# One pool of eight PSUM banks for score pairs and single-bank users, loads ordered on one queue, Q evacuated for both parities in one operation

## The chip, the cores and the metric

The kernel runs on one core of one Trainium2 chip. The metric is the time of one execution on the device in microseconds (us), taken as the median of several runs. Engines are named as in the profile: PE (TensorE matmuls), PEld (its weight loads), DVE (VectorE), ACT (ScalarE), POOL (GpSimd), SP (the queue that issues most loads).

## The reference, cut to what matters

Two branches on an input of 2048 tokens by 512 features, mixed by a gate per token:

```python
g = sigmoid((x * gate_w).sum(-1, keepdims=True))
a = A_ref(x, wqkv, wo)      # attention: 32 heads of 16, causal, window of 256 tokens
b = B_ref(x, w1, b1, w2, b2)     # layernorm, then an MLP over the tokens
return g * a + (1 - g) * b
# A_ref: q, k, v = x @ wqkv; softmax(q k^T / 4, masked) v; @ wo
# B_ref: u = gelu(einsum("bsd,sf->bdf", layernorm(x), w1) + b1); y = einsum("bdf,fs->bds", u, w2) + b2
```

What matters here is the shape of the work. The projections make Q, K and V. Attention runs in 90 *groups*: one block of 128 queries, half the heads, one block of 128 keys. A group is 8 small score matmuls into PSUM, two exps on ACT of 128x1024 each, and 16 small matmuls with V. The MLP has a *first product* (176 matmuls of 512 columns, needs the layernorm of all tokens) and a *second product* (176, needs all of the first and the weight w2, which is loaded into the place of w1 when the first product is over).

## The kernel before

All work is cut into tasks; a planner inside the program (`arrange`) walks through them with assumed durations and fixes one order of instructions for every engine before anything runs. A task may take buffers of a *ring*; the planner decides which buffer of the ring it gets. The framework then puts in the semaphores, from what each instruction reads and writes. So the order is fixed, and an instruction that has to wait holds up everything behind it on its engine.

The parts that the change and the argument touch (cuts marked `# ...`):

```python
    def ring(name, n, shape, dtype, space):
        pool = psum if space == "psum" else sb
        return Ring(name, [pool.tile(shape, dtype, name=f"{name}{i}") for i in range(n)])

    sp = ring("sp", 3, [P, 1024], FP32, "psum")     # three pairs of banks, for scores
    gp = ring("gp", 2, [P, 512], FP32, "psum")      # two single banks, for everything else
    # ...
    def chain(name, mms, deps, prio, piece=2):      # a sum of matmuls, in pieces of two
        b = gp.use()
    # ...
                for p in range(2):                  # Q, once for each parity, on ACT or DVE
                    q.append(copy_out(
                        f"qc{k}_{i}{p}", lambda k=k, p=p: QZ[:, i % NQ, p, k, :], lambda b=b: buf(b)[:],
                        [t, k4] + free_q.get((k, i - NQ), []), 4, b, 0.53, scale=par[:, p:p + 1],
                    ))
    # ...
            b2 = [sp.use(), sp.use()]               # one group takes two of the three pairs
            # ...
            s = add(f"s{qb}.{hf}.{kb}", {"PE": 0.40}, emit_s, need, 1 + 0.001 * slot, takes=b2)
            ex = []
            for j in range(2):
                ex.append(add(
                    f"e{qb}.{hf}.{kb}.{j}", {"ACT": 0.96},
                    lambda j=j, b2=b2, e=e: nc.scalar.activation(
                        out=buf(e)[:, j * 1024:(j + 1) * 1024], in_=buf(b2[j])[:], func=ACT.Exp, scale=SCALE
                    ),
                    [s] + ex, 6 + 0.001 * slot, takes=[e] if j == 0 else [], uses=[b2[j]] + ([e] if j else []),
                ))
```

PSUM is the memory that PE writes its sums to. A *bank* is a piece of it with 512 fp32 values per partition, and both kernels divide PSUM into eight of them: here three pairs and two single banks. Every user of a single bank (transposes, projections, products with V, both MLP products, the output projection) is called a *single* below.

The softmax here doesn't subtract the row's maximum and nothing guards it: scores larger than these inputs give would overflow.

## Time and profile before

270.6 us (269.3 to 271.5). The profiled execution is a slightly longer one, 274.3 us, with a span of 272.2 us on the core. The kernel falls into six stages with different limits. I cut the trace at landmarks: first score matmul, first and last matmul of the first product, first of the second product, last score matmul.

| stage | us | what limits it |
|---|---|---|
| start | 18.7 | loads, then cold matmuls |
| A: projections and attention | 46.3 | DVE, ACT, PE about equally |
| first product | 89.6 | PE |
| wait for w2 | 21.5 | ACT |
| second product | 71.7 | ACT |
| tail | 24.4 | PE alone |

The first fence has the head of the page of the kernel before: the span, and the busy time of each engine.

```profile
span 272.2 us, 6817 instructions
PE 239.9 (88%) x2968; PEld 118.4 (43%) x2968; DVE 145.8 (54%) x256; ACT 214.2 (79%) x255; POOL 68.5 (25%) x50
```

The second has the same kernel by stage: for each stretch its length, then busy time and count of each engine, the granted clock of PE, the share of the DMA engines and GB/s.

```profile
core 0: us, PE busy (x) PEld busy (x) DVE busy (x) ACT busy (x) POOL busy (x), PEclk, DMA share, GB/s
0.00:18.70 18.70, 12.47 (x68) 5.53 (x69) 8.44 (x22) 3.54 (x5) 8.27 (x16) 0.82 0.94 258
18.70:65.00 46.30, 37.46 (x470) 17.86 (x470) 38.21 (x75) 38.12 (x48) 9.74 (x9) 0.93 0.29 110
65.00:154.60 89.60, 84.31 (x1072) 41.71 (x1069) 51.50 (x81) 76.65 (x94) 22.38 (x11) 0.96 0.06 20
154.60:176.10 21.50, 19.03 (x262) 9.91 (x261) 12.07 (x19) 20.21 (x27) 4.01 (x2) 1.00 0.49 186
176.10:247.80 71.70, 67.84 (x981) 34.70 (x981) 29.70 (x50) 69.54 (x78) 22.05 (x11) 1.00 0.06 20
247.80:272.20 24.40, 18.77 (x128) 8.69 (x127) 5.90 (x11) 6.12 (x8) 2.00 (x1) 0.99 0.10 33
```

Read it by rows: in the second product ACT is busy 69.54 of 71.70, and in the last row nobody but PE has much to do. These 18.8 us of PE work come too late.

The third has the waits of PE and ACT of the kernel before that bear on PSUM buffers: who waited for whom, us in total, how often, the longest.

```profile
ACT et L474 <- PE sp L457: 2.7, 6, 1.2
...
PE sp L457 <- ACT et L474: 1.3, 4, 0.5
...
PE gp L356 <- DVE on L534: 4.3, 8, 0.7
PE gp L356 <- ACT QZ L313: 4.2, 5, 1.3
...
PE gp L356 <- DVE QZ L317: 1.7, 3, 0.7
```

The hand-over between scores and exps costs almost nothing (2.7 and 1.3 us in 90 groups). Over all its lines PE waits 14.2 us for DVE and 8.5 us for ACT.

### The profile page before, as it was taken

The page shows a single profiled execution, that of the slowest core. Times are in us where ns is not written, and L with a number is a line of the kernel's source. Part 1 is how long each engine was busy: PE and PEld are TensorE (multiplying, and loading weights), DVE is VectorE, ACT ScalarE, POOL GpSimd, SP SyncE. Part 2 cuts the span into 40 slices and gives each one's busy share as a digit, 9 for nine tenths or more (in the row PEclk, how much of TensorE's full clock was granted, in tenths as well). Part 3 has the DMA queues.
Part 4 walks back from the last instruction along what each step waited for, and adds up shares of the span by engine and source line. Part 5 has one row for each costly group of instructions (what it writes and reads, how often), then busy time and mean ns, then how long its engine had stood idle before and what let it go on. Part 6 is the DMA issues. An engine that isn't in the chain of part 4 may idle for free.

```text
span 272.2 us, 6817 instructions
## 1 busy us (share of the span) xinstructions
PE 239.9 (88%) x2968; PEld 118.4 (43%) x2968; DVE 145.8 (54%) x256; ACT 214.2 (79%) x255; POOL 68.5 (25%) x50
## 2 busy tenths in 40 slices
PE   5588888888989999998798989899998989899894
PEld 1243443434455455444433534445454444444431
DVE  0679977785566554758524574525425253443222
ACT  0239969689988977999569899999999999997221
POOL 8300403041340222131202221133333322222000
PEclk9689979799997999999989999999999999999999
DMA  6999600000000000000000992001001010101001
GB/s 212 214 386 404 235 0 2 1 2 0 2 2 2 0 2 0 2 2 2 1 0 4 363 411 60 0 2 41 4 19 39 5 39 2 41 0 41 22 19 58
DMA packets 9757, 18.00 MB, mean 66 GB/s; under 512 B 672, under 2 KB 5792, under 8 KB 9728
## 3 DMA queue, kind: packets, MB, share of 16 engines
q1 hardware_dynamic: 8512, 15.99, 16.5%
q10 hardware_dynamic: 1056, 1.57, 2.0%
q8 instruction: 23, 0.38, 0.6%
q0 software_dynamic: 160, 0.01, 0.5%
q14 instruction: 6, 0.05, 0.1%
HBM read 15.47 MB, written 2.10 MB: 65 GB/s over the span
## 4 chain that ended last, share of the span: by engine, by line
PE 56%; ACT 20%; DVE 15%; issue 4%; DMA 4%; DVEq 0%; ACTq 0%
PE gp L356 41%; ACT et L474 12%; PE sp L457 7%; PE gp L512 7%; DMA wqkv<-in_A_wqkv_dram 4%; DVE QZ L317 3%; DVE et L483 3%; ACT QZ L313 3%; ACT bp L637 2%; DVE h L423 2%; DVE on L534 2%; DVE ug L611 1%; ACT uf L589 1%; DVE rd L527 1%; PE gp L548 1%
## 5 line engine op out<-in xcount | busy, mean ns | idle before, releaser
L474 ACT ACTIVATE et<-sp 128x1024 bf16<-128x1024 f32 x180 | 171.6, 1045 | 4.2 <-PE sp L457 2.7
L492 POOL TENSOR_SCALAR_AFFINE_SELECT et<-et 128x2048 bf16<-128x2048 bf16 x28 | 56.6, 2021 | 151.7 <-ACT et L474 131.7
L512 PEld LDWEIGHTS <-et 128*128 128x128 bf16 x1440 | 46.1, 96 | 23.6 <-issue 14.2
L483 DVE TENSOR_TENSOR et<-et,mask 128x2048 bf16<-128x2048 bf16 x32 | 39.1, 1223 | 31.5 <-ACT et L474 31.2
L512 PE MATMUL gp<-VA,et 128*128 128x17 bf16 x1440 | 48.2, 171 | 4.2 <-DVE QZ L317 1.1
L356 PE MATMUL gp<-h,wb 128*128 128x512 bf16 (+1 forms) x176 | 47.6, 386 | 0.0
L356 PE MATMUL gp<-ug,wb 128*128 128x512 bf16 (+1 forms) x176 | 44.5, 379 | 2.7 <-DVE on L534 2.6
L356 PEld LDWEIGHTS <-wb 128*128 128x128 bf16 (+2 forms) x352 | 29.9, 98 | 35.2 <-issue 10.9
L356 PE MATMUL gp<-XT,wqkv 128*128 128x512 bf16 x128 | 38.1, 420 | 8.1 <-DMA wqkv<-in_A_wqkv_dram 2.3
L457 PE MATMUL sp<-QZ,KT 32*128 32x256 bf16 x720 | 41.3, 277 | 3.5 <-ACT et L474 1.3
L457 PEld LDWEIGHTS <-KT 32*128 32x128 bf16 x720 | 13.3, 92 | 37.1 <-issue 35.8
L637 ACT ACTIVATE bp<-gp,c,c 128x512 f32<-128x512 f32 x16 | 12.4, 779 | 16.5 <-PE gp L356 16.1
L356 PE MATMUL gp<-wqkv,XT 128*128 128x512 bf16 x64 | 19.3, 407 | 3.8 <-ACT QZ L313 2.5
L527 DVE RECIPROCAL rd<-gp 128x16 f32<-128x16 f32 x32 | 8.1, 254 | 26.0 <-PE gp L512 15.2
L356 PEld LDWEIGHTS <-wqkv 128*128 128x128 bf16 x128 | 11.9, 103 | 22.8 <-issue 13.0
L313 ACT ACTIVATE QZ<-gp,par 128x512 bf16<-128x512 f32 x18 | 12.2, 692 | 10.5 <-DVE QZ L317 6.2
L356 PE MATMUL gp<-wo,xo 128*128 128x512 bf16 x64 | 17.7, 377 | 1.8 <-ACT bp L637 1.0
L645 DVE SCALAR_TENSOR_TENSOR ot<-gp,gg,bp 128x512 bf16<-128x512 f32 x16 | 11.9, 748 | 13.7 <-PE gp L356 12.4
L317 DVE TENSOR_SCALAR QZ<-gp,par 128x512 bf16<-128x512 f32 x14 | 10.5, 750 | 15.2 <-ACT QZ L313 8.8
L594 DVE TENSOR_TENSOR t<-uf 128x512 f32<-128x512 f32 (+1 forms) x11 | 8.1, 738 | 12.3 <-ACT uf L589 12.3
L534 DVE TENSOR_TENSOR on<-gp,rd 128x256 bf16<-128x256 f32 x32 | 13.6, 424 | 1.1
L406 DVE BATCH_NORM_STATS2 stats<-xo 128x6 f32<-128x512 bf16 x16 | 10.4, 681 | 5.5 <-DMA xo<-in_A_x_dram 5.5
(49 smaller groups left out, 129.8 us busy)
## 6 DMA issues: line engine op xcount, KB each, us to landing
wb<-in_B_w_dram SPq DMA_DIRECT2D x4, 1376.0 KB, 17.1
wb<-in_B_w_dram SPq DMA_DIRECT2D x3, 1536.0 KB, 8.0
xo<-in_A_x_dram SPq DMA_DIRECT2D x4, 512.0 KB, 12.9
out_dram<-ot SPq DMA_DIRECT2D x16, 128.0 KB, 1.7
wqkv<-in_A_wqkv_dram ACTq DMA_DIRECT2D x1, 1024.0 KB, 9.8
wqkv<-in_A_wqkv_dram ACTq DMA_DIRECT2D x1, 512.0 KB, 13.3
wo<-in_A_wo_dram SPq DMA_DIRECT2D x1, 512.0 KB, 16.3
wb<-in_B_w_dram SPq DMA_DIRECT2D x1, 512.0 KB, 11.6
```

The lines of the kernel that those rows point to most:

```text
L313: nc.scalar.activation(out_(), in_(), ACT.Copy, scale=scale)
L317: nc.vector.tensor_scalar(out=out_(), in0=in_(), scalar1=scale, scalar2=None, op0=ALU.mult)
L356: nc.tensor.matmul(buf(b)[:rows, :], lhsT=lhsT, rhs=rhs, start=(j == 0), stop=(j == n - 1))
L457: nc.tensor.matmul(buf(b2[r // 2])[:, (r % 2) * 512 + kk * 256:(r % 2) * 512 + kk * 256 + 256], lhsT=KT[32 * r:32 * r + 32, (kb // 4) % NK ...
L474: lambda j=j, b2=b2, e=e: nc.scalar.activation(out=buf(e)[:, j * 1024:(j + 1) * 1024], in_=buf(b2[j])[:], func=ACT.Exp, scale=SCALE),
L483: lambda e=e: nc.vector.tensor_tensor(out=buf(e)[:].rearrange("p (n q) -> p n q", q=P), in0=buf(e)[:].rearrange("p (n q) -> p n q", q=P), ...
L492: lambda e=e: nc.gpsimd.affine_select(out=buf(e)[:], in_=buf(e)[:], pattern=[[0, 16], [-1, P]], compare_op=ALU.is_gt, fill=0.0, base=0, ch ...
L512: nc.tensor.matmul(buf(o)[:, hl * DV:(hl + 1) * DV], lhsT=buf(e)[:, col:col + 128], rhs=VA[:, kb, head, :], start=(first and hl == 0), sto ...
L527: lambda rd=rd, o=o: nc.vector.reciprocal(out=buf(rd)[:], in_=buf(o)[:, 0:16 * DV].rearrange("p (h d) -> p h d", d=DV)[:, :, DH]),
L534: lambda rd=rd, o=o, ob=ob, hf=hf: nc.vector.tensor_tensor(out=buf(ob)[:, hf * 256:(hf + 1) * 256].rearrange("p (h d) -> p h d", d=DH), in ...
L637: lambda bp=bp, b=b, qb=qb: nc.scalar.activation(buf(bp)[:], buf(b)[:], ACT.Identity, bias=c2[:, qb:qb + 1], scale=c1[:, qb:qb + 1]),
L645: lambda bp=bp, b=b, ot=ot, qb=qb: nc.vector.scalar_tensor_tensor(out=buf(ot)[:], in0=buf(b)[:], scalar=gg[:, qb:qb + 1], in1=buf(bp)[:], ...
```

## The change

Its intent: let singles have up to four banks, so that PE always finds a bank for a filler between scores; bring the first loads in sooner; take Q's evacuation off ACT. Four parts:

1. **Pool.** PSUM becomes four tiles of two banks each. A group takes two whole tiles; a single takes one half of tile 2 or 3 (banks 4 to 7).
2. **Loads** go through one queue in the order x0, wqk, x1, wv, x2, x3.
3. **Q** is evacuated by one DVE operation for both parities.
4. **Planner**: an exp is assumed to take 0.905 us, not 0.96; a group may not be planned before the start of the first exp of the group ahead of it; the exp table is loaded at the start.

```diff
-    sp = ring("sp", 3, [P, 1024], FP32, "psum")
-    gp = ring("gp", 2, [P, 512], FP32, "psum")
+    ps = Banks("ps", [0.0] * 8)
+    pst = [psum.tile([P, 1024], FP32, name=f"ps{i}") for i in range(4)]
 ...
     def buf(b):
-        return b.ring.tiles[b.index]
+        if b.ring is not ps:
+            return b.ring.tiles[b.index][:]
+        t = pst[b.index // 2]
+        return t[:] if b.size == 2 else t[:, (b.index % 2) * 512:(b.index % 2 + 1) * 512]
+
+    ANY = (4, 5, 6, 7)
 ...
+    load_x(0)
+    dwk = load_w("wqk", 0, 2 * D, 0.005)
+    load_x(1)
+    dwv = load_w("wv", 2 * D, 3 * D, 0.015)
+    load_x(2)
+    load_x(3)
 ...
-                for p in range(2):
-                    q.append(copy_out(
 ...
+                q = [add(
+                    f"qc{k}_{i}", {"DVE": 1.25},
+                    lambda k=k, b=b: nc.vector.tensor_tensor(
+                        out=QZ[:, i % NQ, :, k, :], in0=buf(b)[:, None, :].to_broadcast([P, 2, SB]),
+                        in1=par[:][:, :, None].to_broadcast([P, 2, SB]), op=ALU.mult,
+                    ),
+                    [t, k4], 4, uses=[b],
+                )]
 ...
-            b2 = [sp.use(), sp.use()]
+            b2 = [ps.use(2), ps.use(2)]
 ...
-            s = add(f"s{qb}.{hf}.{kb}", {"PE": 0.40}, emit_s, need, 1 + 0.001 * slot, takes=b2)
+            s = add(f"s{qb}.{hf}.{kb}", {"PE": 0.40}, emit_s, need, 1 + 0.001 * slot, takes=b2, after=prev)
 ...
-                    f"e{qb}.{hf}.{kb}.{j}", {"ACT": 0.96},
+                    f"e{qb}.{hf}.{kb}.{j}", {"ACT": 0.905},
```

(Cut: the class `Banks`, which prefers low tiles for groups and high banks for singles, and the wait of a projection chain for the last reader of the K or Q that it will replace.)

More of the change, by code (lines that the diff above doesn't have):

```diff
@@ L14, with __init__ @@
 class Buf:
-    def __init__(self, ring):
+    def __init__(self, ring, size=1, banks=None):
         self.ring = ring
+        self.size = size
+        self.banks = banks
         self.index = None
@@ L31, in use, with when, take, give @@
         return Buf(self)
+    def when(self, bufs):
+        times = sorted(x for x in self.avail if x is not None)
+        return times[len(bufs) - 1] if len(times) >= len(bufs) else None
+    def take(self, bufs, start):
+        for b in bufs:
+            b.index = min((i for i, x in enumerate(self.avail) if x is not None), key=lambda i: self.avail[i])
+            self.avail[b.index] = None
+    def give(self, b):
+        self.avail[b.index] = b.end
+class Banks(Ring):
+    def use(self, size=1, banks=None):
+        return Buf(self, size, banks)
+    def when(self, bufs):
+        a = self.avail
+        if bufs[0].size == 2:
+            times = sorted(
+                max(a[i], a[i + 1]) for i in range(0, len(a), 2) if a[i] is not None and a[i + 1] is not None
+            )
+        else:
+            times = sorted(x for i, x in enumerate(a) if x is not None and i in bufs[0].banks)
+        return times[len(bufs) - 1] if len(times) >= len(bufs) else None
+    def take(self, bufs, start):
+        a = self.avail
+        for b in bufs:
+            if b.size == 2:
+                free = [i for i in range(0, len(a), 2) if a[i] is not None and a[i + 1] is not None]
+                b.index = min(free, key=lambda i: (max(a[i], a[i + 1]) > start, i))
+                a[b.index] = a[b.index + 1] = None
+            else:
+                free = [i for i in b.banks if a[i] is not None]
+                b.index = min(
+                    free, key=lambda i: (a[i] > start, a[i ^ 1] is not None and a[i ^ 1] <= start, -i)
+                )
+                a[b.index] = None
+    def give(self, b):
+        for i in range(b.index, b.index + b.size):
+            self.avail[i] = b.end
 class Task:
-    def __init__(self, name, engines, emit, deps=(), prio=50.0, lat=None, takes=(), uses=(), at=0.0):
+    def __init__(self, name, engines, emit, deps=(), prio=50.0, lat=None, takes=(), uses=(), after=()):
         self.name = name
@@ L45, in __init__ @@
             b.users += 1
-        self.at = at
+        self.need = {}
+        for b in self.takes:
+            self.need.setdefault(b.ring, []).append(b)
+        self.after = [(d, s) for d, s in after if d is not None]
         self.done = None
@@ L49, in __init__ @@
         self.next = []
-        self.ready = at
+        self.ready = 0.0
 LATENCY = {"PE": 0.22, "ACT": 0.15, "DVE": 0.12, "POOL": 0.15, "SP": 2.0}
@@ L58, in arrange @@
     for t in tasks:
-        t.left = len(t.deps)
+        t.left = len(t.deps) + len(t.after)
         for d in t.deps:
-            d.next.append(t)
+            d.next.append((t, None))
+        for d, s in t.after:
+            d.next.append((t, s))
     free = {e: 0.0 for e in LATENCY}
@@ L78, in arrange @@
                 start = max(free[e], t.ready)
-                need = {}
-                for b in t.takes:
-                    need[b.ring] = need.get(b.ring, 0) + 1
-                for ring, n in need.items():
-                    times = sorted(x for x in ring.avail if x is not None)
-                    start = max(start, times[n - 1]) if len(times) >= n else None
-                    if start is None:
+                for ring, bufs in t.need.items():
+                    at = ring.when(bufs)
+                    if at is None:
+                        start = None
                         break
+                    start = max(start, at)
                 if start is not None:
@@ L106, in arrange @@
         t.start = start
-        for b in t.takes:
-            ring = b.ring
-            b.index = min(
-                (i for i, x in enumerate(ring.avail) if x is not None), key=lambda i: ring.avail[i]
-            )
-            ring.avail[b.index] = None
+        for ring, bufs in t.need.items():
+            ring.take(bufs, start)
         for b in t.takes + t.uses:
@@ L116, in arrange @@
             if not b.users:
-                b.ring.avail[b.index] = b.end
+                b.ring.give(b)
         order.append(t)
-        for n in t.next:
+        for n, s in t.next:
             n.left -= 1
-            n.ready = max(n.ready, t.done)
+            n.ready = max(n.ready, t.done if s is None else start + s)
             if not n.left:
@@ L210, in buf, with bank @@
     def buf(b):
-        return b.ring.tiles[b.index]
+        if b.ring is not ps:
[3 more added lines that the diff above has]
+    ANY = (4, 5, 6, 7)
+    def bank(banks=ANY):
+        return ps.use(1, banks)
     tasks = []
@@ L218, in add @@
         return t
-    landed = [2.2]
+    landed = [2.3]
     def load(name, emit, kb, q="SP", deps=(), prio=0.0, small=None):
-        landed[0] += kb / 330.0
+        landed[0] += kb / 370.0
         lat = small if small is not None else landed[0]
@@ L228, with load_x, emit, load_w @@
     dx = []
-    dx.append(load("x0", lambda: nc.sync.dma_start(xo[:, 0:4, :], X[0:SB].rearrange("(t p) d -> p t d", p=P)), 512))
-    dwk = load(
-        "wqk",
-        lambda: nc.scalar.dma_start(wqkv[:, :, 0:2 * D], A_wqkv[:, 0:2 * D].rearrange("(c p) n -> p c n", p=P)),
-        1024, q="ACT",
-    )
-    dwv = load(
-        "wv",
-        lambda: nc.scalar.dma_start(wqkv[:, :, 2 * D:3 * D], A_wqkv[:, 2 * D:3 * D].rearrange("(c p) n -> p c n", p=P)),
-        512, q="ACT", prio=0.1,
-    )
-    for i in range(1, NSB):
-        def emit(i=i):
-            nc.sync.dma_start(xo[:, 4 * i:4 * i + 4, :], X[i * SB:(i + 1) * SB].rearrange("(t p) d -> p t d", p=P))
-        dx.append(load(f"x{i}", emit, 512, prio=0.1 * i))
+    def load_x(i):
+        def emit():
+            nc.sync.dma_start(xo[:, 4 * i:4 * i + 4, :], X[i * SB:(i + 1) * SB].rearrange("(t p) d -> p t d", p=P))
+        dx.append(load(f"x{i}", emit, 512, prio=0.01 * len(dx)))
+    def load_w(name, a, z, prio):
+        return load(
+            name, lambda: nc.sync.dma_start(wqkv[:, :, a:z], A_wqkv[:, a:z].rearrange("(c p) n -> p c n", p=P)),
+            z - a, prio=prio,
+        )
+    load_x(0)
[4 more added lines that the diff above has]
+    load_x(3)
     dw1 = []
@@ L297 @@
     k6 = add("biases", {"DVE": 0.35}, biases, [k3], prio=30)
-    wu = gp.use()
+    add("table", {"ACT": 1.4}, lambda: nc.scalar.activation(th[:, 0:1], eps[:, 0:1], ACT.Exp), [k0], prio=0)
+    wu = bank()
     warm = add(
@@ L327 @@
         for c in range(2):
-            b = gp.use()
+            b = bank()
             def emit(i=i, c=c, b=b):
-                g16 = buf(b)[:].bitcast(BF16)
+                g16 = buf(b).bitcast(BF16)
                 for cc in range(2):
@@ L341, with chain @@
                 lambda i=i, c=c: XT[:, 2 * c:2 * c + 2, i * SB:(i + 1) * SB],
-                lambda b=b: buf(b)[:].bitcast(BF16).rearrange("p (c s) -> p c s", c=2),
+                lambda b=b: buf(b).bitcast(BF16).rearrange("p (c s) -> p c s", c=2),
                 [t], 5 + i, b, 0.53, both=False,
             )
-    def chain(name, mms, deps, prio, piece=2):
-        b = gp.use()
+    def chain(name, mms, deps, prio, piece=2, banks=ANY):
+        b = bank(banks)
         n = len(mms)
@@ L383, in project @@
             ]
-            b, t = chain(f"{kind}{k}_{i}", mms, [dwk, xt[i, 0], xt[i, 1], warm], prio)
+            old = free_k.get((k, i - NK), []) if kind == "k" else free_q.get((k, i - NQ), [])
+            b, t = chain(f"{kind}{k}_{i}", mms, [dwk, xt[i, 0], xt[i, 1], warm] + old, prio)
             if kind == "k":
@@ L387, in project @@
                     f"kc{k}_{i}", lambda k=k: KT[:, i % NK, k, :], lambda b=b: buf(b)[:],
-                    [t] + free_k.get((k, i - NK), []), 4, b, 0.53,
+                    [t], 4, b, 0.53,
                 )
             else:
-                q = []
-                for p in range(2):
-                    q.append(copy_out(
-                        f"qc{k}_{i}{p}", lambda k=k, p=p: QZ[:, i % NQ, p, k, :], lambda b=b: buf(b)[:],
-                        [t, k4] + free_q.get((k, i - NQ), []), 4, b, 0.53, scale=par[:, p:p + 1],
-                    ))
+                q = [add(
[6 more added lines that the diff above has]
+                )]
                 qready[k, i] = q
@@ L437 @@
     SCALE = DH ** -0.5
+    LEAD = 0.0
+    prev = []
     slot = 0
@@ L470 @@
             ex = []
+            prev = []
             for j in range(2):
                 ex.append(add(
-                    f"e{qb}.{hf}.{kb}.{j}", {"ACT": 0.96},
+                    f"e{qb}.{hf}.{kb}.{j}", {"ACT": 0.905},
                     lambda j=j, b2=b2, e=e: nc.scalar.activation(
@@ L478 @@
                 ))
+            prev = [(ex[0], LEAD)]
             got = ex
@@ L499 @@
             slot += 1
-        o = gp.use()
+        o = bank()
         last = None
@@ L542 @@
         if len(rel[qb]) == 2:
-            tb = gp.use()
+            tb = bank()
             def emit_t(tb=tb, ob=ob):
@@ L554 @@
             )
-    gb = gp.use()
+    gb = bank()
     def emit_gate():
```

## The prediction

> **What bounds the kernel now.** No one engine throughout. By windows cut at landmarks of the timeline (first score, first and last matmul of the first MLP product, first of the second, last score):
>
> - 0-18.7 us, start: loads. The chain of waits begins with the load of wqkv to 10.6 us. The next 12 matmuls take 0.43 us each, half clock (later 0.22).
> - 18.7-65, projections and attention (A): DVE busy 40 of 46, ACT 40, PE 39.5 (hand-offs of two single banks).
> - 65-154.6, first product: PE 82.
> - 154.6-176, waiting for w2: ACT 20 of 21.5.
> - 176-247.8, second product: ACT 69.5 of 71.7.
> - 247.8-272.2, tail: PE alone, 18.8 of 24.4; five second-product chains are left after the last exp.
>
> Busy (page): PE 239.9, ACT 214.2, DVE 145.8. My sum of warm PE work is 229; some 43 us go to the start, hand-offs and clock (granted 0.96).
>
> **What the change does.**
> 1. Loads: x0, then wqk, then x1, on one queue. Today x0 lands at 7.2 and wqk at 10.6, sharing the engines. At the timeline's 210-290 GB/s x0 should land near 5, wqk near 8.2: 2-2.5 us sooner. The early table load was hidden already.
> 2. Q: 18 ACT (0.69) and 14 DVE (0.75) evacuations become 16 DVE operations, estimated at 1.2 us from the 0.75. ACT loses 12.4 us, DVE gains 9. Today the pair runs in series (waits: DVE on ACT 8.8 us, ACT on DVE 6.2). The Trainium skill, "PSUM — Partial Sum Buffer", Terms, says that two engines may not access one bank at once, reads included; the trace agrees: 1.44 us back to back. The bank is released at most 0.25 us sooner.
> 3. Banks: singles get four banks instead of two; scores mostly the other two pairs. In the built order most score groups reuse pairs 0 and 1, so a group waits for the previous group's second exp; three pairs let it wait for the first only. Estimated 0.6-0.8 us of ACT gap each, unless another ACT operation fills it.
> 4. Order: score groups are held back, fillers come forward. In the built order, groups by stage go from 17/32/8/33 to 29/23/10/28, 512-column matmuls after the last score from 75 to 39.
>
> **On the critical path.** Warm PE work per stage (trace durations) plus losses like today's: start 16.8; A has 62 of PE, 65 of ACT, 65 of DVE: 72; first product 62 of PE: 66; w2 gap, ten groups of exps: 20.5; second product 70.5 of PE, 63.5 of ACT plus gaps: 73.5; tail 10.4 plus 4: 14. Sum near 263. The gain is mainly the tail, about 10 us, and the start, 2; A, with more on DVE, and the two-pair hand-off give some back.
>
> **Predicted 262 us**, range 253 to 269. Faster by over 2%: 0.68; within 2%: 0.28; slower: 0.04.
>
> **What would show it.** First k chain at 8-8.5 us; first exp near 17.5; Q operation 1.15-1.25 us; ACT busy near 201, DVE near 155; first product from 88; last exp 14 us before the end; waits of scores on exps up from 1.3 us, of exps on scores from 2.7, to several us; waits of chains on QZ and on `on` down from 10.
>
> **What would make it wrong.** The two-pair hand-off stalling both PE and ACT on each group (268-275). DVE limiting A, so that the first product starts after 95. Or four single banks removing nearly all PE stalls, with a clock that warms earlier (the skill, "TensorE: Matmul & The Clock Gate", Part 1: about 3.4 us of sustained work; in the trace half clock holds until 15 us): 250.

## More of the kernel before

Each ratio compares a kernel with the kernel before on the same chip in the same rounds; two variants that ran in different rounds are compared by these ratios.

## The result, and the profile after

The changed kernel takes 307.6 us (305.6 to 309.7) against 270.5 us: ratio 1.1375, 95% interval 1.128 to 1.147. It is 37 us slower. (A ratio here is the mean time of one kernel's fast runs over the mean of the other's of the same rounds, so it is not quite the ratio of the medians.)

The page of the changed kernel begins:

```profile
span 308.0 us, 6790 instructions
PE 241.0 (78%) x2921; PEld 122.0 (40%) x2968; DVE 161.0 (52%) x259; ACT 207.2 (67%) x237; POOL 71.9 (23%) x50
```

PE is about as busy as before (241.0 against 239.9 us, though 47 of its 2968 matmuls have no record in this trace), and ACT is less busy. Nearly all of the 36 us of span is waiting: over all lines PE waits 59.4 us, before 27.4. By stage, with the same landmarks:

```profile
core 0: us, PE busy (x) PEld busy (x) DVE busy (x) ACT busy (x) POOL busy (x), PEclk, DMA share, GB/s
0.00:19.40 19.40, 12.47 (x77) 6.62 (x79) 8.91 (x20) 2.68 (x4) 8.28 (x16) 0.91 0.95 264
19.40:113.70 94.30, 68.55 (x884) 34.81 (x898) 62.06 (x109) 60.29 (x70) 19.19 (x13) 0.89 0.13 51
113.70:184.10 70.40, 61.81 (x763) 30.95 (x776) 44.15 (x60) 57.60 (x69) 16.58 (x8) 1.00 0.09 30
184.10:208.40 24.30, 16.12 (x265) 8.83 (x267) 12.94 (x17) 19.36 (x22) 6.16 (x3) 0.75 0.40 151
208.40:290.60 82.20, 71.38 (x861) 35.47 (x876) 29.06 (x48) 63.04 (x69) 19.67 (x9) 0.97 0.06 21
290.60:308.00 17.40, 10.70 (x89) 5.28 (x91) 3.87 (x7) 4.28 (x5) 2.01 (x1) 0.93 0.09 32
```

In stage A no engine is at its limit: 68.55, 62.06 and 60.29 of 94.30. The tail did shrink, as planned, from 24.4 to 17.4 us. The waits that answer to those shown of before (L418 is now the line of the chains, L581 that of the products with V, L524 the scores, L542 the exps):

```profile
ACT et L542 <- PE ps L524: 38.2, 39, 3.3
...
PE ps L418 <- DVE QZ L456: 8.9, 9, 1.9
...
PE ps L418 <- DVE ot L714: 6.1, 9, 1.7
...
PE ps L418 <- DVE on L603: 5.9, 10, 0.8
...
PE ps L581 <- DVE QZ L456: 3.6, 3, 1.5
...
PE ps L524 <- ACT et L542: 2.6, 7, 0.5
```

Over all its lines PE now waits 41.7 us for DVE (before: 14.2) and 13.5 us for ACT (8.5). That is odd: the singles have twice the banks, and PE waits almost three times as long for DVE, which is one of the two engines that read them. The waits of scores on exps stay small (2.6 us), while exps wait 38.2 us for scores.

A stretch of the timeline of the changed kernel, in the first product, shows how odd. Columns: start, length, engine, line, operation, output and input, count, and in brackets the idle time before and what ended it.

```profile
130.67 0.55 PE L581 MATMUL ps<-VA,et 128*128 128x17 bf16 x16
...
131.08 1.96 PE L418 MATMUL ps<-h,wb 128*128 128x512 bf16 x8
131.71 0.26 DVE L596 RECIPROCAL rd<-ps 128x16 f32<-128x16 f32 x1 [0.47 <-PE ps L418]
...
132.32 2.01 POOL L561 TENSOR_SCALAR_AFFINE_SELECT et<-et 128x2048 bf16<-128x2048 bf16 x1 [6.94 <-ACT et L542]
132.65 0.42 DVE L603 TENSOR_TENSOR on<-ps,rd 128x256 bf16<-128x256 f32 x1 [0.68 <-PE ps L418]
...
132.99 1.88 DVE L680 SCALAR_TENSOR_TENSOR ug<-t,uf 128x512 bf16<-128x512 f32 x1
```

The last product with V (L581) ends near 131.2. Its readers are the reciprocal and the multiplication (L596, L603). Neither can start then; both wait for matmuls of the first product (L418), which write another bank. Nothing in the reference makes them depend on each other. What they share is the two-bank tile: in the built program this reciprocal reads the lower half of tile 3 and carries a wait on a matmul of the first product that writes the upper half.

### The profile page after: what moved, and what is told of

Read it like the earlier page. It is cut to its first block, busy times and chain, and to the rows that moved or that the text cites. A ratio compares the mean times of both kernels' runs of the same rounds, so it can differ in the third digit from the quotient of the medians.

```text
span 308.0 us, 6790 instructions
## 1 busy us (share of the span) xinstructions
PE 241.0 (78%) x2921; PEld 122.0 (40%) x2968; DVE 161.0 (52%) x259; ACT 207.2 (67%) x237; POOL 71.9 (23%) x50
## 4 chain that ended last, share of the span: by engine, by line
PE 54%; DVE 25%; ACT 11%; issue 6%; another core or an unknown queue 2%; DVEq 0%; ACTq 0%
PE ps L418 36%; PE ps L581 9%; DVE QZ L456 6%; ACT et L542 5%; PE ps L524 5%; DVE ot L714 4%; DVE on L603 3%; ACT bp L706 2%; DVE et L552 2%; DVE h L488 2%; ACT uf L658 2%; DVE xo L621 1%; DVE rd L596 1%; DVE VA L377 1%
## 5 line engine op out<-in xcount | busy, mean ns | idle before, releaser
L542 ACT ACTIVATE et<-ps 128x1024 bf16<-128x1024 f32 x180 | 174.3, 1025 | 39.0 <-PE ps L524 38.2
L581 PEld LDWEIGHTS <-et 128*128 128x128 bf16 x1440 | 48.1, 97 | 32.0 <-issue 19.9
L581 PE MATMUL ps<-VA,et 128*128 128x17 bf16 x1440 | 50.1, 171 | 10.9 <-DVE QZ L456 3.6
L418 PE MATMUL ps<-ug,wb 128*128 128x512 bf16 (+1 forms) x163 | 46.0, 389 | 7.5 <-DVE ot L714 3.0
L418 PE MATMUL ps<-h,wb 128*128 128x512 bf16 (+1 forms) x164 | 44.4, 379 | 7.2 <-ACT uf L658 4.2
L418 PEld LDWEIGHTS <-wb 128*128 128x128 bf16 (+2 forms) x352 | 30.9, 99 | 46.5 <-issue 24.5
L418 PE MATMUL ps<-XT,wqkv 128*128 128x512 bf16 x117 | 37.6, 431 | 14.7 <-DVE QZ L456 5.5
L552 DVE TENSOR_TENSOR et<-et,mask 128x2048 bf16<-128x2048 bf16 x32 | 38.9, 1219 | 10.5 <-ACT et L542 10.5
L524 PE MATMUL ps<-QZ,KT 32*128 32x256 bf16 x720 | 40.2, 286 | 3.5 <-ACT et L542 2.6
L714 DVE SCALAR_TENSOR_TENSOR ot<-ps,gg,bp 128x512 bf16<-128x512 f32 x16 | 12.0, 751 | 45.2 <-PE ps L418 20.5
L524 PEld LDWEIGHTS <-KT 32*128 32x128 bf16 x720 | 12.2, 93 | 34.8 <-issue 33.8
L456 DVE TENSOR_TENSOR QZ<-ps,par 128x1024 bf16<-128x1024 f32 x16 | 19.5, 1222 | 12.1 <-PE ps L418 6.0
L418 PEld LDWEIGHTS <-wqkv 128*128 128x128 bf16 x128 | 12.5, 106 | 29.8 <-issue 22.7
L418 PE MATMUL ps<-wqkv,XT 128*128 128x512 bf16 x58 | 17.1, 394 | 7.6 <-DVE QZ L456 2.5
L596 DVE RECIPROCAL rd<-ps 128x16 f32<-128x16 f32 x32 | 8.2, 255 | 26.9 <-PE ps L418 16.9
L418 PE MATMUL ps<-wo,xo 128*128 128x512 bf16 x59 | 17.7, 378 | 3.9 <-DVE ot L714 3.1
L603 DVE TENSOR_TENSOR on<-ps,rd 128x256 bf16<-128x256 f32 x32 | 13.6, 425 | 8.7 <-PE ps L418 7.2
L373 ACT ACTIVATE VA<-ps 128x512 bf16<-128x512 f32 x10 | 6.0, 601 | 14.7 <-PE ps L418 8.3
L680 DVE SCALAR_TENSOR_TENSOR ug<-t,uf 128x512 bf16<-128x512 f32 (+1 forms) x11 | 13.9, 1263 | 3.7 <-ACT t L675 3.6
L373 ACT ACTIVATE KT<-ps 128x512 bf16<-128x512 f32 x6 | 3.6, 598 | 17.7 <-PE ps L418 17.1
```

The costliest lines, as they stand in the source:

```text
L418: nc.tensor.matmul(buf(b)[:rows, :], lhsT=lhsT, rhs=rhs, start=(j == 0), stop=(j == n - 1))
L456: lambda k=k, b=b: nc.vector.tensor_tensor(out=QZ[:, i % NQ, :, k, :], in0=buf(b)[:, None, :].to_broadcast([P, 2, SB]), in1=par[:][:, :, N ...
L524: nc.tensor.matmul(buf(b2[r // 2])[:, (r % 2) * 512 + kk * 256:(r % 2) * 512 + kk * 256 + 256], lhsT=KT[32 * r:32 * r + 32, (kb // 4) % NK ...
L542: lambda j=j, b2=b2, e=e: nc.scalar.activation(out=buf(e)[:, j * 1024:(j + 1) * 1024], in_=buf(b2[j])[:], func=ACT.Exp, scale=SCALE),
L552: lambda e=e: nc.vector.tensor_tensor(out=buf(e)[:].rearrange("p (n q) -> p n q", q=P), in0=buf(e)[:].rearrange("p (n q) -> p n q", q=P), ...
L581: nc.tensor.matmul(buf(o)[:, hl * DV:(hl + 1) * DV], lhsT=buf(e)[:, col:col + 128], rhs=VA[:, kb, head, :], start=(first and hl == 0), sto ...
```

## The experiments

Theories before the first runs. **T1, false sharing:** the two halves of a two-bank tile are ordered against each other as if they were one buffer. A read of one half waits for the writes into the other half that stand ahead of it in the program, a write waits for the reads, and a read on DVE waits for a read on ACT. **T2, hand-off:** scores mostly use tiles 0 and 1 (61 of the 90 groups in the built program), so a group can be written only when both exps of the group ahead have read, where three pairs let the first exp suffice. **T3:** the loads, or Q on DVE, cost it.

The built programs already say that T1's waits exist. In the changed kernel the first evacuation of Q on DVE carries a wait on ACT, which at that point reads K out of the other half of the same tile; with a tile for each bank (e1 below) the same instruction waits on PE alone, for its own matmuls:

```
changed kernel   QZ <- ps3   128x2x512   waits: Activation
e1               QZ <- sg2   128x2x512   waits: PE
```

In the trace of the changed kernel the two evacuations stand one behind the other, K on ACT from 9.33 us and Q on DVE from 9.96, `[1.08 <-ACT KT L373]`. A count over the two built programs says the same: of 180 reads of single banks by DVE or ACT, 78 carry a wait on a matmul that writes the other half of the tile in the changed kernel, and none in e1. What such waits cost is for runs to say.

### e1_own: the changed order, a tile for each single bank

```diff
-    pst = [psum.tile([P, 1024], FP32, name=f"ps{i}") for i in range(4)]
+    pst = [psum.tile([P, 1024], FP32, name=f"ps{i}") for i in range(2)]
+    sgl = [psum.tile([P, 512], FP32, name=f"sg{i}") for i in range(4)]
-        return t[:] if b.size == 2 else t[:, (b.index % 2) * 512:...]
+        return pst[b.side][:] if b.size == 2 else sgl[b.index - 4][:]
+            b2[0].side, b2[1].side = 0, 1
```

The planning is untouched, so PE, ACT, DVE and POOL have the same instructions in the same order as in the changed kernel. The price is that groups may no longer use tiles 2 and 3.

> The changed kernel in its own instruction order, but the four single banks are four tiles of their own and score groups always use pair tiles 0 and 1. Theory T1 (two single banks that are halves of one 2-bank tile are ordered against each other as if they were one buffer: a read of one half waits for the writes of the other and the other way round): most of the 37 us goes away, 270-285 us, waits of DVE and ACT evacuations on PE fall. Theory T2 (two-pair hand-off of scores costs it): no gain, since scores use two pairs even more: 305-315 us. Theory T3 (Q on DVE, order of loads): no gain, 300-310 us.

Measured: 281.2 us (279.6 to 281.6), correct, ratio to the kernel before 1.035 (1.032 to 1.038). T1 holds: where the changed kernel was 13.75% above the kernel before, e1 is 3.5% above it, some 26 to 28 of the 37 us gone, although the hand-off has become stricter. By stage (same columns as above; stage A and the second product of e1):

```profile
18.00:92.20 74.20, 62.33 (x886) 33.24 (x900) 63.11 (x109) 60.59 (x70) 17.65 (x13) 1.00 0.19 73
...
187.70:263.50 75.80, 71.24 (x867) 35.33 (x880) 29.54 (x48) 62.97 (x70) 18.85 (x10) 0.96 0.07 22
```

Stage A fell from 94.3 to 74.2 us with the same work in it, the second product from 82.2 to 75.8. PE's waits for DVE fell from 41.7 to 6.6 us in total, its waits of all kinds from 59.4 to 38.2. The two profiled spans differ by more than the medians (308.0 against 277.5 us; one is the longest execution of its kernel, the other the shortest). Of these 30.5 us, 21.2 are waits; another 8.0 are PE's busy time (241.0 against 233.0), for the granted clock was higher too, in stage A 1.00 and not 0.89. What is left is T2's pair of waits; the last line is the largest wait of PE for DVE:

```profile
ACT et L543 <- PE ps L525: 38.4, 70, 1.9
PE ps L525 <- ACT et L543: 26.0, 39, 2.1
...
PE sg L418 <- DVE KT L377: 1.5, 1, 1.5
```

### e2_shared: the kernel before, its two single banks as halves of one tile

```diff
-    gp = ring("gp", 2, [P, 512], FP32, "psum")
+    gpt = psum.tile([P, 1024], FP32, name="gp")
+    gp = Ring("gp", [gpt[:, 0:512], gpt[:, 512:1024]])
```

Same banks in number, same order of instructions, same work. Only the tile that the banks belong to is another.

> The kernel before in its own order, one edit: its two single banks become the two halves of one 2-bank tile. T1: clearly slower, 285-305 us. T2 and T3: unchanged, 268-273 us.

Measured: 396.2 us (394.7 to 397.9), correct, ratio 1.460 (1.455 to 1.465). T1 holds, and the size surprised me: 125 us from naming two banks as one tile, over three times the most that T1 expected. With only one shared tile, every single stands against every other. A few lines of its timeline:

```profile
105.38 0.59 PE L357 MATMUL gp<-h,wb 128*128 128x512 bf16 x2
...
106.01 0.26 DVE L528 RECIPROCAL rd<-gp 128x16 f32<-128x16 f32 x1 [0.47 <-PE gp L357]
...
106.32 0.59 PE L357 MATMUL gp<-h,wb 128*128 128x512 bf16 x2 [0.35 <-DVE rd L528]
...
106.95 0.42 DVE L535 TENSOR_TENSOR on<-gp,rd 128x256 bf16<-128x256 f32 x1 [0.68 <-PE gp L357]
```

The first product and the reciprocal of the attention sums use different banks, yet they take turns: DVE waits for two matmuls, the next two matmuls wait for DVE, DVE waits for those. PE's waits for DVE are 61.7 us in total, for ACT 34.2. The mean granted clock fell to 0.78, so part of the 125 us is slower matmuls and not waiting itself.

That it is the software's ordering and not the memory follows from e1 and from the kernel before: there the same engines work in different banks at once, without these waits and with correct results. The Trainium skill, "PSUM — Partial Sum Buffer", section "PSUM bank collisions raise a hardware error", fits this: two engines collide within one bank, and pairs of accesses to different banks run clean.

### e3_twopairs: the kernel before, scores on two pairs

```diff
     def buf(b):
-        return b.ring.tiles[b.index]
+        return b.ring.tiles[getattr(b, "side", b.index)]
             b2 = [sp.use(), sp.use()]
+            b2[0].side, b2[1].side = 0, 1
```

> The kernel before in its own order, one edit: score groups use pair tiles 0 and 1 alternately instead of three tiles in rotation. T2: 290-310 us, ACT waits of exps on scores 30 us or more. T1 alone: within 275 us.

Measured: 308.2 us (307.5 to 311.4), correct, ratio 1.138 (1.132 to 1.144). So T2 is real too: taking away the third pair alone costs the kernel before as much as the whole change did. In e3 ACT and PE wait for each other, with its own line numbers:

```profile
ACT et L475 <- PE sp L458: 32.8, 55, 1.9
PE sp L458 <- ACT et L475: 30.3, 57, 1.7
```

Three lines of e3's ACT in the second product show the cycle:

```profile
241.35 1.93 ACT L475 ACTIVATE et<-sp 128x1024 bf16<-128x1024 f32 x2
243.73 1.94 ACT L475 ACTIVATE et<-sp 128x1024 bf16<-128x1024 f32 x2 [0.45 <-PE sp L458]
246.11 1.03 ACT L475 ACTIVATE et<-sp 128x1024 bf16<-128x1024 f32 x1 [0.45 <-PE sp L458]
```

and ACT in the kernel before, with three pairs, in its second product, goes without a gap:

```profile
206.10 7.68 ACT L474 ACTIVATE et<-sp 128x1024 bf16<-128x1024 f32 x8
```

In the groups shown ACT idles 0.45 us each: the last six matmuls of the group's scores can start only when the second exp has read, and the next exp waits for them. The second product took 90.2 us in e3 and 71.7 before. But e3 keeps an order that was planned for three pairs; the next runs plan anew.

### e4_own_replan and e13_own_cost: two pairs and four single banks, planned anew

e4 is the changed kernel with the tiles of e1 and a planner that knows that groups have tiles 0 and 1 only. e13 is e4 with one number put back.

```diff
 e4:  -  ... for i in range(0, len(a), 2) if a[i] is not None ...
      +  ... for i in (0, 2) if a[i] is not None ...
 e13: -  f"e{qb}.{hf}.{kb}.{j}", {"ACT": 0.905},
      +  f"e{qb}.{hf}.{kb}.{j}", {"ACT": 0.96},
```

> The changed kernel with tiles of their own for the four single banks and two pair tiles for scores alone, order planned anew. T1: 258-270 us, faster than before. T2: 290 us or more.

> Two pair tiles and four single banks with tiles of their own (e4), with 0.96 us for an exp in the planner. The partner of e11, with the same number and three pairs and two single banks. T2 (two pairs cost more than two more single banks bring): 275-290 us, 10 us or more above e11. If the plan's number was the fault in e4: 263-270 us.

Measured: e4 281.5 us (281.0 to 282.0), ratio 1.037; e13 296.4 us (296.2 to 297.9), ratio 1.095; both correct. For e4 I had expected a kernel faster than before under T1 and 290 or more under T2, and it met neither. e13 lies above its range (275 to 290). With the shared tiles gone (PE waits only 5.5 us for DVE in e4) two pairs still lose, even with a plan made for them: in e4 exps wait 39.4 us for scores and scores 21.3 us for exps, in e13 53.6 and 28.8. In both, mean granted clocks are low (0.86 and 0.84; the kernel before had 0.975 or more in the runs beside them). The low clock is mostly at the end: it was 0.55 in the last 50 us of e4 and 0.50 in the last 71 us of e13, where PE was busy for 31.0 and 45.7 us. So part of what these two lose is slow matmuls, and how much was not separated.

### e5_3pairs_replan and e11_3pairs_cost: everything but the pool

Three pair tiles and two single banks with tiles of their own, as before; loads, Q, table load, holding back of groups kept; planned anew. e11 is e5 with 0.96 us for an exp in the planner.

```diff
+    pst = [... range(3)];  sgl = [... range(2)]
-    ANY = (4, 5, 6, 7)
+    ANY = (6, 7)
 e11: -  {"ACT": 0.905},
      +  {"ACT": 0.96},
```

> The whole change except its pool: three pair tiles for scores and two single banks with tiles of their own, as in the kernel before; loads, Q in one operation, table load, new costs in the planner kept; order planned anew. If false sharing (T1) and the two-pair hand-off (T2) together are the cause, both are gone here: 260-270 us, PE waits on DVE and ACT together under 25 us. If loads or Q (T3) cost something: above 275 us.

> The three-pair version of the change (e5) with one number put back: the planner takes 0.96 us for an exp, as before, not 0.905. If the new cost in the planner is what made e5 6 us slower than e10: 263-267 us. If the holding back of scores, the table load or the moved dependencies did it: 269-272 us.

Measured: e5 270.6 us (269.8 to 270.8), ratio 0.996 (0.992 to 0.999); e11 266.0 us (265.2 to 266.7), ratio 0.982 (0.977 to 0.988). Both correct. In e5 PE waits 24.7 us for DVE and ACT together, as expected (under 25). The pairs of kernels that differ in the pool alone, each planned for its own pool, are now e4 against e5 (ratios to the kernel before 1.037 and 0.996) and e13 against e11 (1.095 and 0.982, same rounds): as built and planned, a third pair of banks for scores is worth 11 to 30 us more than two more banks for singles, the low clock of e4 and e13 included. The shorter exp in the planner costs about 4 us with three pairs (e5 against e11, 0.996 and 0.982), so that number was no improvement there. With two pairs it went the other way (e4 is some 15 us faster than e13); why was not tested, beyond the longer stretch at half clock that e13's trace shows.

### e6_loads, e7_qone, e10_lq: the other parts alone

e6 is the kernel before with the new loads, e7 the kernel before with Q in one operation, e10 with both. Their edits are those parts of the diff above. e6's plan has the same groups in every stage; e7 and e10 were planned anew.

> The kernel before with the loads of the change alone. T3 (loads hurt): over 273 us. Otherwise 267-270 us: wqk lands 3 us sooner, first exp 0-2 us sooner, and not all of that reaches the end.

> The kernel before with Q in one DVE operation alone, order planned anew. T3 (Q on DVE hurts): over 273 us. Otherwise 264-271 us: ACT busy down 12 us, DVE up 9 us.

> The kernel before with loads and Q of the change, pools as before, order planned anew: 262-270 us if the parts that are not the pool are worth what was predicted or a little less; if it lands above 271 us, they bring nothing.

Measured, all correct: e6 268.7 us (ratio 0.989, 0.986 to 0.992), e7 271.7 us (1.000, 0.996 to 1.003), e10 264.7 us (0.975, 0.971 to 0.979). T3 falls: neither part hurts. Loads bring 3 us. e7 is just above its range (264 to 271). Q in one operation brings nothing alone, though ACT's busy time falls from 214.2 to 203.2 us: in the built order six groups move from the first product into stage A and five from the second product into the wait for w2, so exps run ahead and more PE work is left for after the last score: 24.6 us by my sum of warm durations, where the kernel before has 18.2. That this is where ACT's 11 us went fits e12 and e14 below, but was not tested for e7 itself. Together they gain 7 us. What the change has beyond loads, Q and pool (table load, holding back of groups, moved waits) makes no difference that stands clear: e11, which has it, and e10 have overlapping intervals (0.977 to 0.988 and 0.971 to 0.979).

### e12_cost105 and e14_cost110: a version that beats both

e10 too leaves 24.6 us of PE work for after the last score (same sum). A planner that believes exps to be slower plans fewer groups early and more fillers between them. It is one number in e10:

```diff
-                    f"e{qb}.{hf}.{kb}.{j}", {"ACT": 0.96},
+                    f"e{qb}.{hf}.{kb}.{j}", {"ACT": 1.05},     # e12;  e14: 1.10
```

> e10 with a planner that takes 1.05 us for an exp, so that fewer fillers are left for after the last exp (19 us of PE work, not 24.6). If the tail is what is left to win: 259-263 us. If the trace's engines don't follow the plan: 264-267 us.

> e12 with 1.10 us for an exp in the planner: 33 groups of scores in the second product, 11.7 us of PE work after the last exp instead of 19. If the tail is still what is left to win: 256-260 us. If the plan now holds exps back: 261-266 us, with ACT waiting longer for scores.

Measured, both correct: e12 261.1 us (261.0 to 261.4), ratio 0.964 (0.960 to 0.968); e14 258.8 us (258.4 to 259.2), ratio 0.951 (0.945 to 0.956). The second product and the tail of e14, same columns as the stages above:

```profile
164.70:241.20 76.50, 74.06 (x970) 35.81 (x970) 31.11 (x49) 70.54 (x79) 22.11 (x11) 1.00 0.07 22
241.20:257.20 16.00, 11.64 (x138) 6.20 (x137) 4.70 (x9) 4.79 (x6) 2.01 (x1) 0.97 0.10 34
```

PE is busy 74.06 of 76.50 us, and the tail is 16.0 us instead of 24.4. But the shorter tail is not the whole gain: the second product is 4.8 us longer than before, and stage A (39.4 us against 46.3) and the wait for w2 (18.2 against 21.5) are shorter. Against e10, whose tail is 31.7 us, second product and tail together even take 1.1 us more (92.5 against 91.4); fewer groups stand early (17 and 7 in stage A and the wait for w2, not 21 and 13), and PE waits 18.3 us in all instead of 23.2 (before: 27.4). So the times are in the expected ranges, but the gain is not the tail's alone. Less waiting of PE and a short tail are what the change wanted from its pool, and they need no new pool: three pairs, two single banks, the new loads, Q in one operation and a better number.

## Why the prediction was wrong

It gave 262 us (253 to 269); the time is 307.6. The stages that it summed stand here beside the changed kernel and beside e1, which is the changed order without shared tiles (lengths from the windows of each trace):

| stage | predicted | changed kernel | e1 |
|---|---|---|---|
| start | 16.8 | 19.4 | 18.0 |
| A | 72 | 94.3 | 74.2 |
| first product | 66 | 70.4 | 69.7 |
| wait for w2 | 20.5 | 24.3 | 25.8 |
| second product | 73.5 | 82.2 | 75.8 |
| tail | 14 | 17.4 | 14.0 |
| sum | 262.8 | 308.0 | 277.5 |

**The step that failed** is the first half of point 3, "singles get four banks instead of two". The changed kernel has four single banks, but they are two tiles, and the waits follow the tile. So evacuation of one bank and refill of another, which two separate tiles let overlap, take turns wherever the two are halves of one tile. The prediction read the order of instructions off the built program, and the waits that the same program carries (a Q evacuation on DVE waiting for ACT) not closely enough. It forecast "waits of chains on QZ and on `on` down from 10"; they rose to 14.8 us (8.9 and 5.9), and e1 has no such wait of a chain. It also named "four single banks removing nearly all PE stalls" as a risk on the good side; in e1, where they are four in fact, PE's waits for DVE do go down to 6.6 us. Of the 30.5 us between the profiled spans of the two (308.0 and 277.5), 20.1 are in stage A and 6.4 in the second product. The first product, forecast from 88 us on, began at 113.7, in e1 at 92.2. That the effect of shared tiles is at least this large is argued, not shown: e1 also forces every group onto two pairs, which can only add waits.

**The second mis-sized term** is the hand-off. Its gap, "0.6-0.8 us of ACT gap each", was about right (in e3 32.8 us in 55 waits, 0.6 each). Its total was not, where it can be seen alone: "several us" of waits of exps on scores are 38.4 us in e1, and of scores on exps 26.0 us, and the sum of stages had nearly nothing for them. In the changed kernel exps wait 38.2 us for scores too, but scores wait only 2.6 us for exps there, so most of that cannot be laid to the hand-off; scores were late for other reasons, among them PE's 41.7 us of waits for DVE ahead of them. Without shared tiles e1 still is 10 us slower than the kernel before; with three pairs e5 and e11 are not (they have another order and two single banks, though). That the same hand-off cost the changed kernel something is likely, but how much is not shown: e1 puts all groups on two pairs, the changed kernel 61 of 90. The rival, "the two-pair hand-off stalling both PE and ACT" to 268-275 us, was the right direction and too small; e1 (281.2 us), without the shared tiles, is some 6 us above it.

**Loads:** the first k chain began at 7.4 us (predicted 8 to 8.5, before 10.65), but the first exp at 19.8, not 17.5. The trace of the changed kernel shows where it was lost, PE at the start:

```profile
7.40 1.90 PE L418 MATMUL ps<-XT,wqkv 128*128 128x512 bf16 x8 [1.47 <-DVE mv L475]
...
12.38 1.89 PE L396 MATMUL ps<-ident,xo 128*128 128x128 bf16 x16 [3.08 <-DMA xo<-in_A_x_dram]
```

In the fixed order, transposes of x1 stand ahead of the second k and q chains, and x1 comes third on the queue. PE waits 3.1 us for it, and the matmuls of 512 columns after the wait take about 0.43 us again, after 0.24 before it (8 in 1.90 us); the granted clock was 0.50 from 12 to 15 us.

**Q:** the operation takes 1.22 us (predicted 1.15 to 1.25). The groups of lines for it, before and after:

```profile
L313 ACT ACTIVATE QZ<-gp,par 128x512 bf16<-128x512 f32 x18 | 12.2, 692 | 10.5 <-DVE QZ L317 6.2 <-PE gp L356 4.2
...
L317 DVE TENSOR_SCALAR QZ<-gp,par 128x512 bf16<-128x512 f32 x14 | 10.5, 750 | 15.2 <-ACT QZ L313 8.8 <-PE gp L356 6.3
```

```profile
L456 DVE TENSOR_TENSOR QZ<-ps,par 128x1024 bf16<-128x1024 f32 x16 | 19.5, 1222 | 12.1 <-PE ps L418 6.0 <-PE ps L524 4.4 <-ACT KT L373 1.1
```

DVE's addition was 9.0 us (19.5 less 10.5), as predicted. Alone it changed nothing (e7). DVE ended at 161.0 us and not near 155 mostly because other operations on it stretched: those that write `ug`, `t` and `h` take 5.4 us more than before in all. The stretch of timeline in the result has a `ug` operation of 1.88 us, 0.69 elsewhere in the same trace, which ends 0.5 us after the POOL operation beside it. All six `ug` and `t` operations above 1.2 us in this trace end 0.5 us after such a POOL operation. This agrees with the Trainium skill, "SBUF — State Buffer", section "Who interferes with whom", on the ports that DVE and POOL share.

**Right:** the tail. The plan leaves 39 instead of 75 matmuls of 512 columns for after the last score; the tail fell to 17.4 us, and to the predicted 14.0 in e1. The size of stage A without shared tiles (72 against 74.2) was right too.

**Open:** how the remaining 10 us of e1 over the kernel before split between two pairs and the new order, and how much of each wait's cost is the lower granted clock that came with it. Three pairs and four single banks would need ten banks, and both kernels have eight. Whether shared tiles cost less if only one half is used by singles was not run either.

## What to carry to other kernels

A buffer is as free as the unit in which its waits are kept. Before you cut one tile into two buffers, look in the built program whether an access to one half waits for the other half; if it does, give each half a tile of its own, even if the bytes are the same. In this kernel, a third buffer in the busiest hand-off (scores to exps) was worth more than extra places for fillers, and a number in the planner won what a new pool was meant to.

## What the Trainium skill lacked or had wrong

- No page says that waits put in by the framework follow the tile and not the bank. "PSUM — Partial Sum Buffer" advises to guard PSUM by bank and quadrant, or simply by bank; two banks in one tile cost the kernel before 125 us (396.2 against 271.4) with nothing else in the program's order changed, a lower granted clock (0.78) included.
- "TensorE: Matmul & The Clock Gate", Part 1, has the clock fall to half after an idle window of about 3.4 us. In the changed kernel the granted clock was 0.50 from 197 to 212 us, with PE busy at least 1.25 of every 3 us and no wait of PE longer than 1.3 us from 185 us to 212. So this trace shows half clock without an idle stretch of that length; PE had scores and products with V there and few matmuls of 512 columns. A later section of that page, "A second HAM failure mode: psum-queue depth-cycling", has short idle times between groups of matmuls bring the clock down in another kernel, but gives no length or share for them. What exactly brought it down here is not shown.
